# Attention followed by a SoLU layer, batch 0's preparation: 64-bit weights turned into float32 in another way, and the first units placed anew

## The chip, the core and the metric

The kernel runs on one core of a Trainium2 chip. A core has TensorE (PE; its weight loads are counted apart as PEld), VectorE (DVE), ScalarE (ACT), GpSimd (POOL) and SyncE (SP, which issues the DMAs here). Each engine works through its own instructions in a fixed order, and semaphores hold it where it needs another's result. The metric is the device time of one execution, in microseconds.

## The reference

Two attentions in a row: 32 packed tokens per head read the sequence, then the sequence reads the packed tokens. A layer with a SoLU and a layer norm follows. The sizes are batch B = 8, H = 8 heads, S = 576 rows, D = 64.

```python
p_packed = sm_attn(p, k, v)               # softmax(p k^T / 8) v, 32 rows per head
out = sm_attn(q, p_packed, p_packed)      # softmax(q p_packed^T / 8) p_packed
x = out.transpose(0, 2, 1, 3).reshape(4608, 512)
h = x @ w_in                              # 512 x 1024
e = np.exp(h - h.max(-1))
solu = h * e / (e.sum(-1) + 1e-9)
ln = (solu - mean) / np.sqrt(var + 1e-6) * g_ln
result = ln @ w_out                       # 1024 x 512
```

q, k, v, p and g_ln arrive as float32. w_in and w_out arrive as 64-bit floats: 512 x 1024 and 1024 x 512 of them, 4 MB each, seen by the kernel as pairs of 32-bit words (low word, high word).

## The kernel before

**Per batch.** `pack(b)` is the first attention: keys transposed (`kT`), scores on TensorE, softmax, the weights transposed (`e1T`), times v, giving `ppT`. `unpack(b)` is the second one: queries transposed (`qT`), scores, maxima per block of 32 (`mx`), POOL's or DVE's subtraction, an exponential on ACT (`a`), sums (`sm`), a product. It doesn't multiply by the packed values: it computes z = packed x w_in once (`zh`, and the rest `zl`), and the weights of the softmax, transposed (`a2h`, and the rest `a2l`), are then the left operand of `h`. Both are generators, and each `yield` ends a unit.

**Per tile of 128 rows.** `mlp_in` forms h with 12 matmuls (three products of high and low parts, two halves of the heads, two halves of the columns; 24 for a boundary tile, which holds 64 rows of each of two batches), its row maximum `nm` on DVE, an exponential `e` on ACT and u = e x h x a row factor on DVE. `mlp_norm` subtracts the mean and splits the result into two float16 parts `yhl` (the first on ACT, the second on DVE); a transposing DMA on SP makes `yT` of it. `mlp_out` multiplies yT by the scaled w_out (`wch`, and the rest `wcl`, both float16) with 24 matmuls, and DVE brings the result out of PSUM (`o_sb`). Tile i's output product runs some tiles after its h.

**Preparation, before the first tile.** Eight chunks of 128 x 1024 numbers, four of w_in and four of w_out, are turned from 64-bit words into float32, as high part (sign, exponent, 23 bits) and low part. `high_part` takes the high word: ACT scales it as a float32 by 2^-112 (L202), DVE shifts it by 3 and clears the sign bit (L204), and DVE puts the sign back (L205). `add_low_part` isolates the exponent on DVE (L212) and multiplies the low word by it, on DVE (L217) or on ACT and then POOL or DVE (L220, L221); the sum is formed on POOL or DVE (L233), or on TensorE as two products with an identity (L226, L227), which ACT copies back (L229). A digit of `HOW` per chunk says how: 0 for DVE alone up to 6. `prepare_w_out` then takes magnitudes on ACT (`mag`), sums them on TensorE, makes a power of two per column from the sum (`scale`, `inv`), scales by it and by g_ln (L321 on ACT, L322 on POOL or DVE), casts to float16 (L323) and takes the residual (L330).

**What sets the order.** A scheduler places each unit by its position in the program, shifted by the offset of the `high_priority` around it. Tables of offsets do this for batch 0's preparation (`PACK0`, `W_IN`, `UNPACK0`, `W_OUT`, `SCALE_AT`, `PARTS`). `FIRST_BATCH` says behind which tile of batch 0 each unit of batch 1's unpacking and batch 2's packing stands, and with which offset; `LATER` does so for the other batches. `LOADS` is the order of the first loads (w a chunk of w_in, o one of w_out, P the packed tokens of the later batches), and `FETCH` places the loads of later batches. All loads, transposing DMAs and stores are issued by SP in one queue. From batch 1 on TensorE's order is that of the program.

Buffers: `e`, `u`, `o_sb`, `zh`, `zl`, `yhl`, `yT` have two each, `mag` one, the PSUM tile `pa` three, `h` two. The raw words of w_in and of two chunks of w_out lie in the tiles `zh` and `zl`, those of the other two in `raw`, which k and q share (three of them).

## Time and profile before

| | |
|---|---|
| median of 3 runs | 468.33 us (467.21 to 469.08) |
| the profiled execution | 468.75 us, span 466.9 us |
| granted TensorE clock, mean | 0.952 |
| busy TensorE (PE) | 429.6 us, 92% of the span |
| busy VectorE (DVE) | 355.1 us, 76% |
| weight loads (PEld) | 236.3 us, 51% |
| busy ScalarE (ACT) | 231.2 us, 50% |
| busy GpSimd (POOL) | 143.4 us, 31% |

Shares are over the whole span, and the first 150 us differ from the rest: there the weights are prepared and batch 0 and half of batch 1 are set up, and the engines take turns as the one that is waited for. So what follows reads stretches of the span and single marks in it. A group's row gives line, engine, operation, output and inputs, partitions x elements, count, then busy time and mean ns of one, then idle time ahead of it and what ended it.

### The profile page before, as it was taken

The numbers are of one execution on the slowest core, as the hardware profiler recorded it, in microseconds if no ns is written. First come the engines' busy times: TensorE is split into PE (matmuls) and PEld (weight loads), VectorE is DVE, ScalarE is ACT, GpSimd is POOL, SyncE is SP. The second block draws the span as 40 slices with busy tenths as digits, with TensorE's granted clock in tenths as the row PEclk, the third lists the DMA queues.
The fourth block names the chain that finished last, engine by engine and source line by source line (L and its number), as shares of the span: only waits on it lengthen the run. The fifth ranks groups of instructions, "written<-read, shape, count | busy, mean of one in ns | idle before, by whom it ended". The sixth has DMA issues, their size and how long they took to land.

```text
span 466.9 us, 8257 instructions
## 1 busy us (share of the span) xinstructions
PE 429.6 (92%) x3116; PEld 236.3 (51%) x3116; DVE 355.1 (76%) x649; ACT 231.2 (50%) x403; POOL 143.4 (31%) x243
## 2 busy tenths in 40 slices
PE   9698577977978999999999999999999999999995
PEld 7472235733344455456644554566445545565542
DVE  4567999887774998998489989984898687566651
ACT  3477747763341556366346563663466444444430
POOL 2325467923200513321015123210152242212220
PEclk9889657898997999999999999999999999999999
DMA  9999999999949949989969489357433324435442
GB/s 267 338 268 286 155 191 132 128 184 173 153 103 186 142 97 160 224 128 157 176 140 144 97 155 183 77 119 178 69 67 69 76 62 113 90 67 125 80 115 65
DMA packets 237880, 67.00 MB, mean 143 GB/s; under 512 B 208912, under 2 KB 231440, under 8 KB 237328
## 3 DMA queue, kind: packets, MB, share of 16 engines
q1 hardware_dynamic: 237840, 66.48, 75.8%
q8 instruction: 24, 0.39, 0.4%
q14 instruction: 16, 0.13, 0.1%
HBM read 37.23 MB, written 9.44 MB: 100 GB/s over the span
## 4 chain that ended last, share of the span: by engine, by line
PE 38%; DVE 31%; ACT 9%; issue 7%; DMA 7%; POOL 4%; SPq 2%; DVEq 0%; POOLq 0%; ACTq 0%
PE po L564 21%; PE h L521 12%; DVE nm L523 4%; ACT yhl L544 3%; DMA zh<-in_moe_w_in_dram 3%; DVE qT L428 3%; DVE kT L350 3%; DVE u L534 3%; DVE zl L500 3%; ACT e L549 2%; DVE yhl L545 2%; DVE mx L443 2%; DVE sm L448 2%; PE pa L407 1%; PE pa L467 1%
## 5 line engine op out<-in xcount | busy, mean ns | idle before, releaser
L564 PE MATMUL po<-wch,yT 128*128 128x512 f16 x576 | 182.7, 382 | 5.9 <-DVE o_sb L566 4.8
L564 PEld LDWEIGHTS <-yT 128*128 128x128 f16 x864 | 81.0, 98 | 115.2 <-issue 24.7
L564 PE MATMUL po<-wcl,yT 128*128 128x512 f16 x288 | 109.7, 381 | 0.0
L521 PE MATMUL h<-zh,a2h 128*128 128x512 f32 x160 | 70.2, 439 | 1.8 <-DVE u L534 1.5
L531 ACT ACTIVATE e<-h,nm 128x1024 f32<-128x1024 f32 x36 | 40.1, 1115 | 58.1 <-DVE nm L523 57.6
L544 ACT ACTIVATE yhl<-u,negmu 128x1024 f16<-128x1024 f32 x36 | 41.4, 1149 | 50.9 <-POOL negmu L542 47.2
L521 PE MATMUL h<-zh,a2l 128*128 128x512 f32 x160 | 64.4, 403 | 0.0
L521 PE MATMUL h<-zl,a2h 128*128 128x512 f32 x160 | 64.2, 401 | 0.0
L545 DVE SCALAR_TENSOR_TENSOR yhl<-u,negmu,yhl 128x1024 f16<-128x1024 f32 x36 | 46.4, 1288 | 17.4 <-ACT yhl L544 17.3
L534 DVE SCALAR_TENSOR_TENSOR u<-e,s_row,h 128x1024 f32<-128x1024 f32 x36 | 46.0, 1277 | 9.8 <-ACT e L531 8.6
L523 DVE TENSOR_REDUCE nm<-h 128x1 f32<-128x1024 f32 x36 | 43.6, 1212 | 11.7 <-PE h L521 11.6
L566 DVE SCALAR_TENSOR_TENSOR o_sb<-po,c_row,inv 128x512 f32<-128x512 f32 x36 | 26.8, 745 | 26.1 <-PE po L564 26.1
L551 POOL TENSOR_SCALAR s_eps<-se,s_row 128x1 f32<-128x1 f32 x36 | 10.7, 297 | 102.2 <-ACT e L531 65.3
L554 POOL TENSOR_SCALAR c_row<-sq,s_eps 128x1 f32<-128x1 f32 x36 | 15.7, 437 | 82.9 <-ACT e L549 82.9
L549 ACT ACTIVATE e<-u,negmu 128x1024 f32<-128x1024 f32 x36 | 40.9, 1136 | 0.0
L521 PEld LDWEIGHTS h<-zh,a2h 128*128 128x128 f32 x160 | 31.1, 194 | 18.9 <-issue 9.0
L521 PEld LDWEIGHTS h<-zh,a2l 128*128 128x128 f32 x160 | 30.8, 193 | 7.9 <-issue 0.5
L521 PEld LDWEIGHTS h<-zl,a2h 128*128 128x128 f32 x160 | 31.1, 194 | 6.0
L444 POOL TENSOR_TENSOR s<-s,mx 128x576 f32<-128x576 f32 x14 | 16.0, 1160 | 49.3 <-DVE mx L443 49.3
L446 ACT ACTIVATE a<-s 128x576 f32<-128x576 f32 x16 | 10.9, 684 | 30.6 <-POOL s L444 28.1
L508 DVE TENSOR_TENSOR a2l<-s,a2h 128x576 fp32r<-128x576 f32 x16 | 14.0, 881 | 13.1 <-ACT a2h L507 13.1
L381 ACT ACTIVATE e<-pa,nmx 128x288 f32<-128x288 f32 x28 | 13.7, 496 | 19.4 <-DVE nmx L373 10.8
(139 smaller groups left out, 614.1 us busy)
## 6 DMA issues: line engine op xcount, KB each, us to landing
out_dram<-o_sb SPq DMA_DIRECT2D x36, 256.0 KB, 2.1
v_sb<-in_v_dram SPq DMA_DIRECT2D x16, 512.0 KB, 6.0
raw<-in_k_dram SPq DMA_DIRECT2D x28, 288.0 KB, 6.4
raw<-in_q_dram SPq DMA_DIRECT2D x96, 72.0 KB, 2.8
zh<-in_moe_w_in_dram SPq DMA_DIRECT2D x2, 1024.0 KB, 7.0
zl<-in_moe_w_in_dram SPq DMA_DIRECT2D x2, 1024.0 KB, 8.4
raw<-in_q_dram SPq DMA_DIRECT2D x4, 512.0 KB, 9.3
raw<-in_moe_w_out_dram SPq DMA_DIRECT2D x2, 1024.0 KB, 6.0
```

The costliest lines, as they stand in the source:

```text
L350: nc.vector.transpose(out=kT[:, g], in_=kraw[:, g].rearrange('p a i -> p (a i)'))
L444: eng.tensor_tensor(out=s2[r], in0=s2[r], in1=mx.unsqueeze(2).broadcast_to([P, NB, J]), op=ALU.subtract)
L521: nc.tensor.matmul(h[:, 512 * n:512 * n + 512], lhsT=lhsT, rhs=z[:, r, 512 * n:512 * n + 512], start=t == 0, stop=t == len(terms) - 1)
L523: nc.vector.tensor_reduce(out=nm, in_=h, axis=AX.X, op=ALU.max, negate=True)
L531: nc.scalar.activation(e, h, AF.Exp, bias=nm, accum_out=se)
L534: nc.vector.scalar_tensor_tensor(out=u, in0=e, scalar=s_row, in1=h, op0=ALU.mult, op1=ALU.mult, accum_out=su)
L544: nc.scalar.activation(yhl[:, 0], u, AF.Identity, bias=negmu)
L545: nc.vector.scalar_tensor_tensor(out=yhl[:, 1], in0=u, scalar=negmu, in1=yhl[:, 0], op0=ALU.add, op1=ALU.subtract)
L549: nc.scalar.activation(e, u, AF.Square, bias=negmu, accum_out=sq)
L554: nc.gpsimd.tensor_scalar(out=c_row, in0=sq, scalar1=1.0 / DF, scalar2=s_eps, op0=ALU.mult, op1=ALU.add)
L564: nc.tensor.matmul(po, lhsT=yT[:, a, c], rhs=w[:, c], start=c == 0 and t == 0, stop=c == NFC - 1 and t == 2)
L566: nc.vector.scalar_tensor_tensor(out=o_sb, in0=po, scalar=c_row, in1=inv, op0=ALU.mult, op1=ALU.mult)
```

## The change

The high part takes two full-width instructions instead of three: ACT scales by 2^-112 with Prelu, whose slope for negative inputs is 2^32, and DVE shifts the bits by 3; the slope leaves the sign bit where the shift puts it in its place. `low_part` makes the exponent out of ACT's bits with a shift and a mask in one DVE instruction (L209), and multiplies it by the low word, on DVE for six chunks (L211, `HOW` 'd') or on ACT (L213, in place) and POOL (L214) for two ('p'). The sum of high and low part is formed on TensorE for all eight chunks (`whole`, L224 and L225), where it was for three. ACT copies it back for w_in (L579) and for four of the eight pieces of w_out (L301). The other four, marked 'x' in `SCALED_BY`, DVE scales by both factors straight out of PSUM (L313). The residuals of w_out (L323) are all on DVE, where three were on POOL; of the scalings that aren't 'x', two are on POOL instead of seven. The low parts of the last two chunks get a tile of their own (`spare_rest`, of the tag `zl`). All tables of batch 0 have new numbers.

```diff
-HOW = '42313324'
-SCALED_BY = 'pppppdpp'
-REST_BY = 'pdddppdd'
-ZL_BY = 'pppp'
-A2L_BY = 'dd'
+HOW = 'dddddpdp'
+SCALED_BY = 'dppxxpxx'
+REST_BY = 'dddddddd'
+ZL_BY = 'pppd'
+A2L_BY = 'dp'
...
-FIRST_BATCH = [[3, 3, 3, 5, 6, 11, 15], [6, 6, 8, 8, 10, 15, 16, 16, 16], ...
+FIRST_BATCH = [[1, 2, 2, 2, 4, 4, 12], [9, 12, 14, 20, 20, 20, 21, 24, 24], ...
...
-FETCH = [[['k', 0, 0], ['v', 0, 0], ['q', 0, 0]], ...
+FETCH = [[['k', 0, 500], ['v', 0, 500], ['q', 1, -200]], ...
...
         bits = mlp.tile([P, DF], F32, name='e', bufs=2)
-        nc.scalar.activation(bits, hi.bitcast(F32), AF.Copy, scale=2.0 ** (-112))
-        bits = bits.bitcast(I32)
-        nc.vector.tensor_scalar(out=bits, in0=bits, scalar1=3, scalar2=2147483647, op0=ALU.logical_shift_left, op1=ALU.bitwise_and)
-        return nc.vector.scalar_tensor_tensor(out=dst.bitcast(I32), in0=hi, scalar=-2147483648, in1=bits, op0=ALU.bitwise_and, op1=ALU.bitwise_or)
+        nc.scalar.activation(bits, hi.bitcast(F32), AF.Prelu, scale=2.0 ** (-112), alpha=2.0 ** 32)
+        nc.vector.tensor_scalar(out=dst.bitcast(I32), in0=bits.bitcast(I32), scalar1=3, scalar2=None, op0=ALU.logical_shift_left)
+        return bits
+
+    def low_part(bits, raw, chunk, rest):
         lo, _ = words_of(raw)
-        ...
+        nc.vector.tensor_scalar(out=bits.bitcast(I32), in0=bits.bitcast(I32), scalar1=3, scalar2=-8388608, op0=ALU.logical_shift_left, op1=ALU.bitwise_and)
+        if HOW[chunk] == 'd':
+            nc.vector.scalar_tensor_tensor(out=rest, in0=lo.bitcast(U32), scalar=2.0 ** (-52), in1=bits, op0=ALU.mult, op1=ALU.mult)
+        else:
+            nc.scalar.activation(lo.bitcast(F32), lo.bitcast(U32), AF.Copy, scale=2.0 ** (-52))
+            EN(nc, HOW[chunk]).tensor_tensor(out=rest, in0=lo.bitcast(F32), in1=bits, op=ALU.mult)
+        return rest
...
+    def whole(high, rest, i):
+        half = slice(512 * i, 512 * i + 512)
+        ps = ps_a.tile([P, 512], F32, name='pa')
+        nc.tensor.matmul(ps, lhsT=ident, rhs=high[:, half], start=True, stop=False)
+        nc.tensor.matmul(ps, lhsT=ident_r, rhs=rest[:, half], start=False, stop=True)
+        return ps
...
             with tc.high_priority(offset=W_OUT[n][2]):
-                add_low_part(wg[n], w_out_raw[n], 4 + n, g_sb[:, 2 * n:2 * n + 2])
+                rests[n] = low_part(rests[n], w_out_raw[n], 4 + n, rest_tile() if n < 2 else spare_rest[:, n - 2])
+                for i in range(2):
+                    if SCALED_BY[2 * n + i] != 'x':
+                        w = wg[n][:, i * DM:(i + 1) * DM]
+                        nc.scalar.activation(w, whole(wg[n], rests[n], i), AF.Copy, scale=g_sb[:, 2 * n + i:2 * n + i + 1])
...
-                if how == 's' and (not scaled):
-                    nc.vector.scalar_tensor_tensor(out=w, in0=w, scalar=g_sb[:, c:c + 1], in1=scale, op0=ALU.mult, op1=ALU.mult)
+                if SCALED_BY[c] == 'x':
+                    nc.vector.scalar_tensor_tensor(out=w, in0=whole(wg[c // 2], rests[c // 2], c % 2), scalar=g_sb[:, c:c + 1], in1=scale, op0=ALU.mult, op1=ALU.mult)
                 else:
-                    ...
+                    EN(nc, SCALED_BY[c]).tensor_tensor(out=w, in0=w, in1=scale, op=ALU.mult)
```

**Where the instructions stand.** First SP's queue, before, from the third chunk of w_out on: v and k of batch 1 (`v_sb`, `raw`), packed p (`pT`), q of batch 1.

```order
L138 DMA raw<-in_moe_w_out_dram 128x2x1024
L138 DMA zh<-in_moe_w_out_dram 128x2x1024
L107 DMA v_sb<-in_v_dram 128x8x128 x2
L134 DMA v_sb<-in_v_dram 64x8x64
L96 DMA raw<-in_k_dram 32x72x32 x4
L272 DMA pT_84<-p2t 64x896 x4
L107 DMA raw<-in_q_dram 128x8x128 x2
L115 DMA raw<-in_q_dram 64x4x64 x2
```

SP's queue after, from the same place:

```order
L138 DMA raw<-in_moe_w_out_dram 128x2x1024
L107 DMA v_sb<-in_v_dram 128x8x128 x2
L134 DMA v_sb<-in_v_dram 64x8x64
L138 DMA zh<-in_moe_w_out_dram 128x2x1024
L265 DMA pT_84<-p2t 64x896 x4
L96 DMA raw<-in_k_dram 32x72x32
L107 DMA raw<-in_q_dram 128x8x128
L96 DMA raw<-in_k_dram 32x72x32
L107 DMA raw<-in_q_dram 128x8x128
L115 DMA raw<-in_q_dram 64x4x64
L96 DMA raw<-in_k_dram 32x72x32 x2
L115 DMA raw<-in_q_dram 64x4x64
```

The last chunk of w_out moved behind v, and the four parts of k moved behind packed p and between the parts of q. Ahead of this stretch, w_out's first chunk moved from behind q of batch 0 to ahead of it.

ACT before, from the high part of w_in's last chunk (read from `zl`) on; L398 copies the packing weights of batch 0, L128 and L129 its queries:

```order
L202 ACTIVATE e<-zl 128x1024
L220 ACTIVATE u<-zh 128x1024
L398 COPY e1T<-pa 64x256
L398 COPY e1T<-pa 128x512
L128 COPY qT<-h 128x2x2x128
L129 COPY qT<-h 128x64
L128 COPY qT<-h 128x2x2x128
L129 COPY qT<-h 128x64
L202 ACTIVATE e<-raw 128x1024
```

ACT after, from the same instruction on:

```order
L202 ACTIVATE e<-zl 128x1024
L390 COPY e1T<-pa 128x512
L390 COPY e1T<-pa 64x256
L213 ACTIVATE zh<-zh 128x1024
L579 COPY w_in_sb<-pa 128x512
L260 ACTIVATE p2raw<-p2raw 128x896
L579 COPY w_in_sb<-pa 128x512
L128 COPY qT<-h 128x2x2x128
L129 COPY qT<-h 128x64
```

The low part of w_out's second chunk (L213) moved ahead of the copies of w_in, the scaling of packed p (L260) and the copies of the queries.

DVE before, around the first output tile (`o_sb`, L566); L439, L443 and L448 belong to the unpacking of batch 1:

```order
L439 STREAM_TRANSPOSE s_889<-pa 128x288
L439 STREAM_TRANSPOSE s_890<-pa 128x288
L545 SCALAR_TENSOR_TENSOR yhl<-u,negmu,yhl 128x1024
L439 STREAM_TRANSPOSE s_889<-pa 128x288
L443 TENSOR_REDUCE mx<-s_889 128x18
L545 SCALAR_TENSOR_TENSOR yhl<-u,negmu,yhl 128x1024
L566 SCALAR_TENSOR_TENSOR o_sb<-po,c_row,inv 128x512
L439 STREAM_TRANSPOSE s_890<-pa 128x288
L428 STREAM_TRANSPOSE qT<-raw 128x576 x4
```

DVE after, from the first output tile on:

```order
L558 SCALAR_TENSOR_TENSOR o_sb<-po,c_row,inv 128x512
L515 TENSOR_REDUCE nm<-h 128x1
L407 COPY ppT<-pa 128x128
L517 TENSOR_SCALAR bound<-nm 128x1
L518 TENSOR_SCALAR bound<-nm,bound 128x1
L520 RECIPROCAL s_row<-bound 128x1
L526 SCALAR_TENSOR_TENSOR u,su<-e,s_row,h 128x1024
L537 SCALAR_TENSOR_TENSOR yhl<-u,negmu,yhl 128x1024
L431 STREAM_TRANSPOSE s_878<-pa 128x288
L431 STREAM_TRANSPOSE s_879<-pa 128x288
L431 STREAM_TRANSPOSE s_878<-pa 128x288
L558 SCALAR_TENSOR_TENSOR o_sb<-po,c_row,inv 128x512
```

The first output tile moved ahead of the unpacking's transposes, of a row maximum and of a yhl; the second one stands among the transposes now, where the first one stood.

From about the row maximum of the boundary tile between batches 0 and 1 on, the orders of both kernels are the same: of the changed kernel's instructions these are the last 2561 of 3184 on TensorE, 442 of 616 on DVE, 179 of 298 on ACT and 192 of 231 on POOL. The table of activation functions is loaded once in both.

More of the change, by code (lines that the diff above doesn't have):

```diff
@@ L201, in high_part @@
         bits = mlp.tile([P, DF], F32, name='e', bufs=2)
-        nc.scalar.activation(bits, hi.bitcast(F32), AF.Copy, scale=2.0 ** (-112))
-        bits = bits.bitcast(I32)
-        nc.vector.tensor_scalar(out=bits, in0=bits, scalar1=3, scalar2=2147483647, op0=ALU.logical_shift_left, op1=ALU.bitwise_and)
-        return nc.vector.scalar_tensor_tensor(out=dst.bitcast(I32), in0=hi, scalar=-2147483648, in1=bits, op0=ALU.bitwise_and, op1=ALU.bitwise_or)
-    def add_low_part(dst, raw, chunk, factors=None):
-        how = HOW[chunk]
-        lo, _ = words_of(raw)
-        power = mlp.tile([P, DF], F32, name='u', bufs=2)
-        nc.vector.tensor_scalar(out=power.bitcast(I32), in0=dst.bitcast(I32), scalar1=-8388608, scalar2=None, op0=ALU.bitwise_and)
-        rest = power
-        if how in '36':
-            rest = mlp.tile([P, DF], F32R, name='u', bufs=2)
-        if how in '026':
-            nc.vector.scalar_tensor_tensor(out=rest, in0=lo.bitcast(U32), scalar=2.0 ** (-52), in1=power, op0=ALU.mult, op1=ALU.mult)
-        else:
-            low = rest if how == '3' else mlp.tile([P, DF], F32, name='u', bufs=2)
-            nc.scalar.activation(low, lo.bitcast(U32), AF.Copy, scale=2.0 ** (-52))
-            EN(nc, 'd' if how in '45' else 'p').tensor_tensor(out=rest, in0=low.bitcast(F32) if how == '3' else low, in1=power, op=ALU.mult)
-        if how in '36':
-            for i in range(2):
-                half = slice(512 * i, 512 * i + 512)
-                ps = ps_a.tile([P, 512], F32, name='pa')
-                nc.tensor.matmul(ps, lhsT=ident, rhs=dst[:, half], start=True, stop=False)
-                nc.tensor.matmul(ps, lhsT=ident_r, rhs=rest[:, half], start=False, stop=True)
-                if factors is None:
-                    nc.scalar.copy(dst[:, half], ps)
-                else:
-                    nc.scalar.activation(dst[:, half], ps, AF.Copy, scale=factors[:, i:i + 1])
-        else:
-            EN(nc, 'p' if how in '124' else 'd').tensor_tensor(out=dst, in0=dst, in1=rest, op=ALU.add)
@@ L330, in prepare_w_out @@
                     EN(nc, REST_BY[c]).tensor_tensor(out=wcl[:, c], in0=w, in1=wch[:, c], op=ALU.subtract)
-        return last.ins
     def pair(b):
@@ L582, in packed_attention_solu_kernel @@
         with tc.high_priority(offset=W_IN[g][0]):
-            high_part(w_in_sb[:, g], w_in_raw[g], g)
+            bits = high_part(w_in_sb[:, g], w_in_raw[g], g)
         with tc.high_priority(offset=W_IN[g][1]):
-            add_low_part(w_in_sb[:, g], w_in_raw[g], g)
+            bits = low_part(bits, w_in_raw[g], g, rest_tile())
+            for i in range(2):
+                nc.scalar.copy(w_in_sb[:, g, 512 * i:512 * i + 512], whole(w_in_sb[:, g], bits, i))
+    spare_rest = par.tile([P, 2 * DF], F32R, name='zl', bufs=2).rearrange('p (n f) -> p n f', n=2)
     keep_busy(*BUSY[1])
```

33 lines of the change are left out of this document (15 added, 18 removed).

## The prediction

> **What bounds the kernel now.** I read first the busy time by stretches (columns: length; busy PE, weight load, DVE, ACT, POOL with their counts; granted clock; DMA share; GB/s).
>
> ```profile
> 36.00:48.00 12.00, 9.56 (x75) 2.40 (x74) 10.12 (x11) 9.75 (x12) 7.44 (x3) 1.00 1.01 290
> 48.00:60.00 12.00, 7.03 (x12) 2.67 (x11) 12.00 (x17) 9.49 (x16) 5.75 (x4) 0.64 1.18 165
> 60.00:72.00 12.00, 8.93 (x44) 4.52 (x44) 11.96 (x16) 5.45 (x10) 5.78 (x4) 0.50 1.14 176
> 300.00:400.00 100.00, 99.07 (x730) 54.10 (x728) 77.20 (x151) 50.71 (x89) 25.64 (x58) 1.00 0.42 91
> ```
>
> From 300 to 400 us TensorE is busy 99.07 of 100: there only its work counts, and the change leaves that work and its order alone. From 48 to 72 us DVE is busy 23.96 of 24 and PE idles 8: the preparation is bound by DVE. So the change is worth what it moves the moment at which batch 0 hands over. Second came the chain of waits, for marks on the way there (start, length, what), and one ACT row.
>
> ```profile
> 62.61 2.67 DVE kT L350 x4
> 95.88 4.65 DMA yT<-yhl
> 112.37 0.76 DVE o_sb L566
> 133.79 1.23 DVE nm L523
> ```
> ```profile
> 109.93 1.15 ACT L544 ACTIVATE yhl<-u,negmu 128x1024 f16<-128x1024 f32 x1 [3.71 <-DMA yT<-yhl]
> ```
>
> The marks: K, where batch 1's keys are transposed on DVE (62.6); T, where the first tile's transposed activations have landed (95.88 + 4.65 = 100.5); O, where the first output tile has left PSUM and the second output product may start (112.37 + 0.76 = 113.1); N, the maximum over the boundary tile (133.8). After N the orders are the same, so the shift of N is the forecast. O is late because its DVE instruction stands behind a yhl that waits, through ACT (idle 3.71), for a transposing DMA.
>
> **The change on DVE.** Its prices are taken from undisturbed instructions (the first fence: line, operation, count, busy, mean ns, idle before):
>
> ```profile
> L204 DVE TENSOR_SCALAR e<-e 128x1024 int32<-128x1024 int32 x8 | 7.2, 894 | 8.7 <-ACT e L202 8.7
> L212 DVE TENSOR_SCALAR u<-w_in_sb 128x1024 int32<-128x1024 int32 x4 | 2.8, 695 | 2.3 <-POOL u L221 2.3
> L205 DVE SCALAR_TENSOR_TENSOR w_in_sb<-zh,e 128x1024 int32<-128x1024 int32 x2 | 2.5, 1225 | 0.1
> L221 POOL TENSOR_TENSOR u<-u 128x1024 fp32r<-128x1024 f32 (+1 forms) x4 | 10.2, 2550 | 22.5 <-ACT u L220 15.0 <-DVE sm L449 6.2 <-DVE mx L443 1.3
> L322 POOL TENSOR_TENSOR yhl<-yhl,o_sb 128x512 f32<-128x512 f32 x4 | 6.6, 1671 | 3.3 <-DVE o_sb L310 3.3
> ```
> ```profile
> 45.82 2.38 POOL L221 TENSOR_TENSOR u<-u 128x1024 fp32r<-128x1024 f32 x1 [1.27 <-DVE mx L443]
> 46.08 3.19 DVE L205 SCALAR_TENSOR_TENSOR yT<-raw,e 128x1024 int32<-128x1024 int32 x1
> 93.53 0.67 DVE L330 TENSOR_TENSOR wcl<-yhl,wch 128x512 f16<-128x512 f32 x1
> 34.82 0.28 DVE L415 COPY ppT<-pa 128x128 f32<-128x128 f32 x1
> 83.92 1.23 DVE L534 SCALAR_TENSOR_TENSOR u<-e,s_row,h 128x1024 f32<-128x1024 f32 x1
> ```
>
> A chunk costs DVE 0.69 + 1.23 + 0.69 now and 2 x 0.69 after: 8 x 1.23 = 9.8 saved. Low-part products on DVE go from 4 to 6: +2.5. Four scalings out of PSUM are new (between 0.67, all in SBUF, and the 0.76 of o_sb, out of PSUM; I take 0.74, its nearest kin): +3.0. Residuals on DVE go from 5 to 8: +2.0; one zl comes, one a2l goes. Sum: -2.3 us of clean work.
>
> The larger part is POOL. It loses 9 full-width instructions, 4 scalings, 3 residuals and one zl, and gets 2 low products and one a2l: 9 x 2.55 + 8 x 1.67 - 2 x 2.55 - 1.67 = 29.5 us less. What this gives DVE: the L205 at 46.08 took 3.19 instead of 1.23 while POOL ran from 45.82 to 48.20, and the eight L204 have a mean of 0.894 against 0.695. The Trainium skill (SBUF — State Buffer, "Who interferes with whom") says that a VectorE instruction with two SBUF inputs and a GpSimd instruction that reads SBUF exclude each other for a whole instruction; 48.20 + 1.23 = 49.43 against the measured end 49.27, so this trace agrees.
>
> Both parts together, counted on the queue. From the copy of ppT (ends 35.1) to the end of the first u (85.15) DVE has now 50 us, nearly all busy. After, the same stretch holds all eight residuals (three now) and full width 4 x 1.23 + 8 x 0.69 + a p2t of about 1.1 + nm 1.23 + u 1.23 = 14.0, 33 instructions of 512 or 576 columns at 0.67 (three scale steps at an estimated 0.4, four scalings at 0.74) = 21.6, seven of 288 at about 0.4 = 2.8, ten tiny ones about 1: 39 us. If DVE never waited, the u would end 11 us earlier. It will wait:
>
> **What is late next.** ACT and the queue of loads (SP), each in order.
>
> ```profile
> 35.86 1.13 ACT L202 ACTIVATE e<-zh 128x1024 f32<-128x1024 f32 x1 [1.31 <-DMA zh<-in_moe_w_out_dram]
> 37.51 0.56 ACT L229 COPY w_in_sb<-pa 128x512 f32<-128x512 f32 x1
> 49.98 0.68 ACT L446 ACTIVATE a<-s 128x576 f32<-128x576 f32 x1 [2.48 <-DVE s L444]
> 26.00:28.00 2.00, 2.00 (x35) 1.50 (x33) 1.41 (x2) 2.00 (x4) 0.35 (x1) 0.65 0.37 21
> ```
> ```profile
> 36.58 0.40 SPq L138 DMA_DIRECT2D zh<-in_moe_w_out_dram  x1
> zh<-in_moe_w_out_dram SPq DMA_DIRECT2D x1, 1024.0 KB, 9.1
> 40.38 5.16 SPq L134 DMA_DIRECT2D v_sb<-in_v_dram  x1
> v_sb<-in_v_dram SPq DMA_DIRECT2D x1, 128.0 KB, 9.9
> 51.58 1.63 SPq L96 DMA_DIRECT2D raw<-in_k_dram  x1
> raw<-in_k_dram SPq DMA_DIRECT2D x1, 288.0 KB, 6.4
> 61.55 0.65 SPq L115 DMA_DIRECT2D raw<-in_q_dram  x1
> raw<-in_q_dram SPq DMA_DIRECT2D x1, 64.0 KB, 4.3
> ```
>
> On ACT the low part of w_out's second chunk (in zh, landed at 35.86) now stands ahead of the w_in copies, the scaling of p and all q copies: ACT idles from about 27.4 until that load. Behind it, by widths at 0.5 to 1.05 from start to start: eight w_in copies 4.0, four signs (Prelu) 4.2, two low parts 2.1, p 0.9, q copies 2.5, magnitudes 2.5, w_out copies 1.9: 18.1 us; then about 2 us of waiting for the last w_out chunk, which now comes after v (v cost 50.3 - 45.7 = 4.6 us of queue). So batch 0's softmax exponentials start at 54 to 56 instead of 49.98, and DVE reaches the keys at about 60.5 instead of 62.6. Prelu itself is in no row: between the copy's 1.13 and, say, twice that; I take 1.13, as the same words pass; at twice, four lie in this chain, +4.5 us, of which the next wait hides 3.5.
>
> The keys are not there. Now they land at 51.58 + 6.4 = 58.0, ahead of packed p and q, whose last part lands at 61.55 + 4.3 = 65.85. After, their four parts stand behind packed p and between the four of q; only a 64 KB part of q is behind them. Equal bytes in a queue that is full end them at 65.85, less the gap of 26 to 28 us (21 GB/s now), which is likely filled, as w_out's first chunk is issued ahead of q: 64.0 to 65.9. I take 64.0: **K moves by +1.4**, and DVE's relief up to there is gone.
>
> From K to the end of u: 22.5 us now. After: 20.4 of the 39 us, 2.3 for a loop (a2l on DVE, four matmuls in queue, the last magnitude, then DVE's scale), 1.5 for three POOL scalings beside it (5.0 us of POOL; 0 to 5.0): 24.2. End of u: 88.2, +3.0.
>
> **Given back behind u.** SP and PE prices:
>
> ```profile
> 73.35 8.99 SPq L85 DMA_DIRECT2D raw<-in_q_dram  x12
> 90.30 5.48 SPq L85 DMA_DIRECT2D raw<-in_q_dram  x6
> 95.88 3.08 SPq L547 DMA_TRANSPOSE yT<-yhl  x1
> 33.88 1.02 PE L226 MATMUL pa<-w_in_sb,ident 128*128 128x512 f32 x2
> 34.97 1.02 PE L226 MATMUL pa<-w_in_sb,ident 128*128 128x512 f32 x2
> 143.94 0.63 PE L521 MATMUL h<-zh,a2l 128*128 128x512 f32 x1
> ```
>
> No residual is left after u. nm and batch 2's keys take 4.4 us, then three q parts on SP (0.75 to 0.91 each, 2.5), then the transposing DMA: T = 88.2 + 4.4 + 2.5 + 4.65 = 99.75, -0.8. The second transpose follows after 3.1 + 8 x 0.83 = 9.7 us and lands at 109.4. The first output tile no longer stands behind the waiting yhl: its 24 products end before that, so O = 109.4, -3.7.
>
> From O to N: 20.7 now, all PE work. After, batch 1's unpacking scores stand behind 22 of the second product's 24 matmuls; from there a chain of o_sb, maximum, four q transposes, second maximum, POOL's subtraction, exponential, sums, POOL's product, transpose and a2l ends 20.9 us after O, and 13 matmuls at 0.23 follow: 23.9, +3.2. Sum: 1.4 + 1.6 - 3.8 - 2.9 + 3.2 = **-0.5 us at N**.
>
> Ten identity pairs more on PE (34.97 - 33.88 = 1.09 each, 10.9 us) cost nothing: PE waits in that stretch for ACT and DVE, 10.5 us from 36 to 72 as it is; were that cover gone, up to 10.9.
>
> The profiled execution took 468.75 us, 0.42 above the median 468.33. So 468.75 - 0.5, less 0.42: **467.8 us**.
>
> **Rivals.** (1) The relief arrives, faster. If the keys land before DVE reaches them (60.5), the wait of 3.5 us goes: 464.3; if the unpacking also hides behind PE's 20.7 us, another 3.2: 461. For it: SP's queue had a gap. Against: the rows of the queue above. (2) The keys later, slower: every us after 64.0 moves N one to one, at 66.9 the run is 2.8 us longer than my forecast, out of the band; with 68 it is 471.8. For it: the parts of q ahead of them; against: equal bytes. (3) POOL's three scalings block DVE's in-order queue for their whole 5.0 us instead of 1.5: 471.3. The L205 row speaks for it, that some of DVE's operands there are in PSUM against it; it decides from 2.8 us lost. By the rule of SBUF — State Buffer in the Trainium skill, this is the price where both operands of DVE's instruction are in SBUF. (4) PE idles about 5 us ahead of the 13 matmuls, and they run at 0.43 as the one at 143.94 (0.63 with its pipeline, next start 0.43 later) does: +2.6, 470.4. The Trainium skill (TensorE: Matmul & The Clock Gate, "Part 1") says an idle window of about 3.4 us halves the clock; the 0.50 of 60 to 72 us agrees.
>
> **How the numbers follow.** About 0.5% (2.3 us: 466.0 to 470.7) is what this measurement can tell from no change. Forecast 0.32 (own range 466 to 470); rival 1 0.40, in two steps of 0.22 and 0.18, each less likely than the forecast; rival 2 0.15; rival 3 0.09; rival 4 0.04, inside the band. Faster 0.40, same 0.36, slower 0.24. The range leaves out a part of the 461 and what goes past 472: 460.5 to 472.5.
>
> **What would show it.** DVE waits some 3 us for batch 1's keys, which start at 64 to 66; ACT idles from 27 to 35; POOL under 20 us up to 100; the first transposed tile lands near 99.8, the second product starts near 109.4, N comes near 133.3. It is wrong if the keys start below 61 or above 67, if Prelu rows are not near 1.13, or if PE is busy all through the unpacking.

## The result: slower by 0.8%, and the profile after

The changed kernel takes 472.55 us (median of 9 runs, 470.48 to 474.40), the kernel before 468.41 us (9 runs, 467.21 to 471.00). The ratio is 1.0081, with a 95% interval from 1.0053 to 1.0108: 4.1 us slower. The forecast was 467.8 us, half a microsecond faster than before, with a range of 460.5 to 472.5; the time lies 0.05 us above the range. The profiled execution, 470.48 us with a span of 468.6 us, is the fastest of its nine. A second profile of the same code (472.99 us, span 470.4 us) is nearer to the median, and stands beside it where the difference matters.

First the busy time by stretches, the same ones as before (columns: length; busy PE, weight load, DVE, ACT, POOL; granted clock; DMA share; GB/s).

```profile
26.00:28.00 2.00, 2.00 (x57) 1.42 (x60) 1.39 (x2) 0.85 (x3) 0.00 (x0) 0.50 1.21 292
36.00:48.00 12.00, 10.59 (x59) 5.19 (x58) 7.19 (x9) 10.48 (x21) 0.88 (x1) 1.00 1.07 309
48.00:60.00 12.00, 11.51 (x77) 4.05 (x76) 10.57 (x17) 9.38 (x15) 2.37 (x2) 1.00 1.11 195
60.00:72.00 12.00, 7.49 (x28) 4.01 (x28) 8.35 (x12) 6.27 (x11) 8.01 (x5) 0.76 1.45 145
300.00:400.00 100.00, 99.07 (x729) 54.34 (x727) 78.18 (x155) 50.63 (x88) 25.59 (x59) 1.00 0.44 92
```

The stretch from 300 to 400 us is as it was. From 48 to 72 us DVE is busy 18.92 of 24 us, where it was busy 23.96: its relief is there, and turned into waiting. POOL does 34 us up to 156 us, where it did 64. Now the marks on DVE and SP in the timeline (start, length, engine, line, instruction, idle time ahead and what ended it):

```profile
64.96 2.76 DVE L342 STREAM_TRANSPOSE kT<-raw 128x576 f32<-128x576 f32 x4 [2.60 <-issue]
73.83 0.69 DVE L304 TENSOR_SCALAR o_sb<-po 128x512 f32<-128x512 f32 x1 [2.89 <-PE po L295]
86.87 1.27 DVE L526 SCALAR_TENSOR_TENSOR u<-e,s_row,h 128x1024 f32<-128x1024 f32 x1
93.90 2.05 SPq L539 DMA_TRANSPOSE yT<-yhl  x1
108.36 0.75 DVE L558 SCALAR_TENSOR_TENSOR o_sb<-po,c_row,inv 128x512 f32<-128x512 f32 x1 [4.13 <-PE po L556]
137.15 1.22 DVE L515 TENSOR_REDUCE nm<-h 128x1 f32<-128x1024 f32 x1 [0.70 <-PE h L513]
149.42 1.23 DVE L515 TENSOR_REDUCE nm<-h 128x1 f32<-128x1024 f32 x1 [3.64 <-PE h L513]
```

Batch 1's keys (K) start at 65.0 instead of 62.6, the column scale's first step at 73.8 instead of 69.8, the first u at 86.9 instead of 83.9, the first output tile (O) leaves PSUM at 109.1 instead of 113.1, and the boundary tile's maximum (N) comes at 137.15 instead of 133.79. The next row maximum, the last row here, came at 147.80 before and comes at 149.42.

That last pair gives the shortest account of the result. Up to this maximum both kernels have done the same products, except that the changed one has summed ten more pieces on TensorE (30 matmuls). One row each for before and after, from the start to that maximum:

```profile
0.00:147.80 147.80, 118.24 (x953) 68.31 (x961) 109.93 (x181) 79.57 (x145) 61.64 (x64) 0.85 1.05 197
```
```profile
0.00:149.42 149.42, 125.23 (x983) 71.52 (x991) 96.58 (x182) 74.99 (x142) 32.82 (x50) 0.90 1.02 192
```

TensorE's busy time grew by 6.99 us and its idle time fell by 5.37 (29.56 to 24.19): 1.62 us later. The second profile of the changed code has 125.23 us busy and 25.92 idle, and comes to this maximum at 151.15, 3.35 us later than before. Behind this maximum all 20 profiles of this study take 319.1 to 319.9 us to the end, so it is a mark that can be compared between the kernels.

### The profile page after: what moved, and what is told of

Its sections match the earlier page's. It is cut to its first block, busy times and chain, and to the rows that moved or that the text cites. A ratio compares the mean times of both kernels' runs of the same rounds, so it can differ in the third digit from the quotient of the medians.

```text
span 468.6 us, 8288 instructions
## 1 busy us (share of the span) xinstructions
PE 436.6 (93%) x3146; PEld 239.6 (51%) x3146; DVE 341.9 (73%) x650; ACT 226.6 (48%) x400; POOL 114.4 (24%) x229
## 4 chain that ended last, share of the span: by engine, by line
PE 38%; DVE 34%; ACT 9%; SPq 8%; issue 7%; DMA 3%; POOL 1%; DVEq 0%; ACTq 0%
PE po L556 18%; PE h L513 12%; DVE nm L515 4%; DVE kT L342 4%; ACT yhl L536 4%; DVE qT L420 3%; SPq L107 3%; DVE u L526 3%; DVE zl L492 3%; DVE yhl L537 2%; ACT e L541 2%; DVE sm L440 2%; DVE mx L363 2%; DVE mx L435 2%; SPq L115 1%
## 5 line engine op out<-in xcount | busy, mean ns | idle before, releaser
L513 PEld LDWEIGHTS h<-zh,a2h 128*128 128x128 f32 x160 | 31.5, 197 | 22.6 <-issue 7.1
L389 PE MATMUL pa<-ident,e 128*128 128x128 f32 (+1 forms) x80 | 15.0, 324 | 7.9 <-ACT e L373 7.7
```

Of the source, the lines that this page charges most:

```text
L513: nc.tensor.matmul(h[:, 512 * n:512 * n + 512], lhsT=lhsT, rhs=z[:, r, 512 * n:512 * n + 512], start=t == 0, stop=t == len(terms) - 1)
```

## The experiments

All ratios are against the kernel before, run on the same chip in the same comparison. Over the six comparisons the median of the kernel before was 467.96 to 468.89 us, so a difference of times from two comparisons can be off by about 1 us for this alone. Ten of the eighteen measured times lie outside every range that was stated for them: these runs rule theories out more than they confirm one.

**1. Again, and the tables taken back.** The changed code as it is; the changed code with the old `FIRST_BATCH`; and with nine tables of numbers old. In the third kernel the arithmetic, the letters that say which engine does what, and `LOADS`, the order of the first loads (the first chunk of w_out ahead of batch 0's queries), are still new.

```diff
-FIRST_BATCH = [[1, 2, 2, 2, 4, 4, 12], [9, 12, 14, 20, 20, 20, 21, 24, 24], ...
+FIRST_BATCH = [[3, 3, 3, 5, 6, 11, 15], [6, 6, 8, 8, 10, 15, 16, 16, 16], ...
 (third kernel: PACK0, W_IN, UNPACK0, W_OUT, SCALE_AT, CHUNKS, PARTS, FETCH old too)
```

> The changed kernel itself, unchanged, for a second trace: the profiled execution shown took 470.48 us, the fastest of nine with a median of 472.55. If what the trace shows (+1.7 us at the row maximum of the second tile behind the boundary, 149.4 against 147.8) is the whole effect, the median comes out near 470.5 here. If single executions lose another 2 us in stretches that PE runs at half clock, the median is 472 to 473 again, and a profiled execution above 472 has longer such stretches before 150 us, with the same order and the same wait elsewhere.

> The changed kernel with the old table of where batch 0's tiles take the units of batch 1's unpacking and batch 2's packing. Theory placement: the loss was made behind the first u, where the unpacking of batch 1 came late and PE waited and ran at half clock; with the old table 468 to 470. Theory preparation: the loss was made ahead of the first tile (keys at 65.0 instead of 62.5, first u at 88.2 instead of 85.2); the table changes nothing, 472 to 473.

> The changed kernel's new arithmetic with all nine tables of batch 0's placement old: the arithmetic alone. Theory placement: near the kernel before or faster, 464 to 468, since DVE has 2.3 us and POOL 29.5 us less work. Theory preparation: the new arithmetic with its waits on ACT and its late magnitudes costs by itself, 471 to 475.

Measured: 472.96 us (1.0097 [1.0066, 1.0129]), 480.90 us (1.0295 [1.0259, 1.0332]) and 481.13 us (1.0277 [1.0238, 1.0316]). The result repeats. The new arithmetic with the old tables is 13.2 us slower than the kernel before (481.13 less the 467.96 of the same comparison), and `FIRST_BATCH` alone carries nearly all of the difference between the tables (480.90 against 481.13). With the old tables N itself is hardly later than in the changed kernel (137.72 against 137.15), but the next maximum comes 20.6 us behind it instead of 12.3; a row of TensorE in the timeline of the kernel with all tables old shows the wait between them:

```profile
142.75 2.47 PE L389 MATMUL pa<-ident,e 128*128 128x128 f32 x9 [4.13 <-ACT e L373]
```

There the packing of batch 2 starts behind N, and TensorE waits for its exponentials. So N alone is not a safe finishing line: what stands right behind it has to be read with it.

**2. A warm TensorE ahead of the boundary tile.** Ten products more, whose result is overwritten, keep TensorE busy in the wait ahead of it.

```diff
+                if warm_first and n == 0 and t == 6:
+                    for _ in range(WARM):
+                        nc.tensor.matmul(h[:, 512:1024], lhsT=terms[0][0], rhs=zl[1][:, 0, 512:1024], start=True, stop=True)
```

> The changed kernel with ten extra products of TensorE ahead of batch 1's share of the boundary tile (their result is overwritten), in the stretch where PE idles from 125.9 to 128.2 us and then runs at half clock until 134.7. Theory half clock: the 18 products behind the idle stretch and the two groups among them go from 8.9 to about 7 us, the row maximum behind them from 137.2 to about 135.2, and 1 to 2 us are won at the end, 470.5 to 471.5. Theory preparation: what counts is the chain through DVE, no gain: 472 to 473.

Measured: 472.04 us (1.0076 [1.0048, 1.0103]). In the changed kernel TensorE idles 2.27 us ahead of these products, and they then start about 0.43 us apart until 134.3, and 0.23 apart behind that:

```profile
128.19 0.80 PE L513 MATMUL h<-zh,a2h 128*128 128x512 f32 x1 [2.27 <-ACT a2h L499]
131.05 0.63 PE L513 MATMUL h<-zh,a2h 128*128 128x512 f32 x1
131.47 0.63 PE L513 MATMUL h<-zl,a2h 128*128 128x512 f32 x1
134.67 0.40 PE L513 MATMUL h<-zh,a2l 128*128 128x512 f32 x1
134.91 0.39 PE L513 MATMUL h<-zh,a2h 128*128 128x512 f32 x1
```

With the ten products the boundary tile runs at 0.23, and N comes 1.7 us earlier than in the second profile (137.17 against 138.88), though the keys start as late there (66.10). But the next stretch, which is slow in the changed kernel too (144.8 to 148.3), is slow for longer (145.0 to 150.6):

```profile
127.99 2.56 PE L517 MATMUL h<-zl,a2h 128*128 128x512 f32 x10
135.93 0.39 PE L518 MATMUL h<-zh,a2l 128*128 128x512 f32 x1
147.21 0.63 PE L518 MATMUL h<-zh,a2l 128*128 128x512 f32 x1
147.63 0.63 PE L518 MATMUL h<-zh,a2h 128*128 128x512 f32 x1
```

The half clock cost N about 1.7 us; counted from O it was 2.1 (25.9 us from O to N, against 28.0 in both profiles of the changed kernel). The next maximum comes 14.1 us behind N instead of 12.3, so nearly all of it is lost again, and the run is 0.9 us faster than the changed kernel in the same comparison, within the intervals.

**3. Batch 1's keys earlier, and later, in SP's queue.**

```diff
-        prefetch(1, what, 0)
+        prefetch(1, what, 600 if what == 'k' else 0)      # keys first
+        prefetch(1, what, 400 if what == 'q' else 0)      # keys last
```

> The changed kernel with the four parts of batch 1's keys issued ahead of its queries on SP (DVE's transposes of them then stand ahead of the second half of batch 0's softmax; else the same order). Theory keys: DVE's wait for the keys carries the loss, and from the keys on to the row maximum of the second tile behind the boundary both kernels take the same 84.5 to 85.3 us. Here the keys start near 61.5 instead of 65.0 to 66.4, and 2 to 4 us are won: 468.5 to 470.5. Theory downstream: the loss comes from the order behind the first u and from half-clock stretches, an earlier start is eaten up there: 472 to 473.

> The changed kernel with the queries of batch 1 ahead of the last three parts of its keys on SP; on DVE only two instructions behind the keys change places. Theory keys: the keys land 0.5 to 3 us later than in the changed kernel, and the end moves by as much, 473 to 476. Theory downstream: no change, 472 to 473.

Measured: 471.89 us (1.0083 [1.0052, 1.0115]) and 473.33 us (1.0096 [1.0072, 1.0120]). With the keys first, DVE starts them at 59.94 instead of 64.96 to 66.39, and the first row maximum comes at 75.33 instead of 75.77 to 77.58: 5 to 6.5 us of keys moved it by 0.4 to 2.2 us. So issuing the keys first, on which the forecast's first term rested, doesn't win back the 4 us. It doesn't price the keys' landing alone, though: with the keys first DVE's transposes of them also stand ahead of the second half of batch 0's softmax. The run with the keys last prices nothing: its keys start at 65.30, between the 64.96 and 66.39 of the two profiles of the changed kernel, and that its time lies in the range of the theory "keys" is chance. One reason why earlier keys are worth little stands in TensorE's timeline of the changed kernel, and in DVE's row of the first piece that is read out:

```profile
78.61 1.13 PE L224 MATMUL pa<-yhl,ident 128*128 128x512 f32 x2
79.17 0.80 PE L225 MATMUL pa<-zl,ident_r 128*128 128x512 f32 x1
79.90 0.93 PE L360 MATMUL pa<-kT,pT 64*32 64x288 f32 x16
```
```profile
76.90 0.74 DVE L313 SCALAR_TENSOR_TENSOR yhl<-pa,g_sb,o_sb 128x512 f32<-128x512 f32 x1
```

The sums of the 'x' pieces (L224, L225) lie in the PSUM tiles `pa` until DVE has the column scale and reads them out. There are three such tiles, and the packing scores of batch 1 (L360) need them: they start at 79.90, 15 us behind their keys. Before, they started right behind them:

```profile
63.35 2.96 PE L368 MATMUL pa<-kT,pT 64*32 64x288 f32 x17 [3.07 <-DVE kT L350]
```

**4. The two halves of the change, each alone.** The kernel before with all nine new tables; the kernel before with the old tables and only the high part by Prelu and a shift; and the new tables with the Prelu part.

```diff
-        nc.scalar.activation(bits, hi.bitcast(F32), AF.Copy, scale=2.0 ** (-112))
-        ...
+        nc.scalar.activation(bits, hi.bitcast(F32), AF.Prelu, scale=2.0 ** (-112), alpha=2.0 ** 32)
+        return nc.vector.tensor_scalar(out=dst.bitcast(I32), in0=bits.bitcast(I32), scalar1=3, scalar2=None, op0=ALU.logical_shift_left)
```

> The kernel before, its old arithmetic, with the nine new tables of placement (the loads of batch 1 keep the old order on SP: keys ahead). If the new tables are the better placement whatever the arithmetic, 465 to 468. If they only suit the arithmetic they came with, over 472, as the old tables under the new arithmetic (481).

> The kernel before with one part of the change alone: Prelu and one shift make the high part, eight times 1.2 us less on DVE; low parts, sums and tables are the old ones. If DVE's work ahead of the keys bounds the old kernel as its trace says, and the placement holds, up to 5 us faster: 463 to 467. If a shorter instruction only lets DVE wait for the next load or for POOL's sums, 467 to 469; if the scheduler's placement falls apart as it did for the whole arithmetic under the old tables, over 472.

> The old arithmetic with the new tables (463.8 us), and of the new arithmetic Prelu and the shift alone. If the 9.8 us that DVE no longer works are on the path there, 459 to 462; if DVE only waits longer for POOL and for loads, 463 to 465; if the scheduler's order gets worse as under the old tables (+3.3), over 466.

Measured: **463.80 us (0.9899 [0.9863, 0.9934])** for the new tables alone, the fastest kernel of this study; 471.65 us (1.0066 [1.0040, 1.0092]) for Prelu with the old tables; 466.08 us (0.9951 [0.9935, 0.9968]) for Prelu with the new ones. So the placement gains 4.6 us and the rest of the change loses 8.8 (472.6 less 463.8), of which the Prelu part is 2.3; by the intervals each of these two losses is uncertain by about 2 us. The rest is called the arithmetic below, but it holds two things more: the letters that hand work from one engine to another, and the place of w_out's first chunk in `LOADS`, which is old in the kernels with the old arithmetic and new in those with the new one. No run takes `LOADS` back alone. That it does something can be seen: in the changed kernel TensorE waits 0.70 us for batch 0's queries (`raw<-in_q_dram`) at 30.82, and in the kernel before it doesn't wait for them. The same window as above, for the new tables alone:

```profile
0.00:142.65 142.65, 118.41 (x953) 69.76 (x961) 106.03 (x180) 79.63 (x145) 63.02 (x64) 0.84 1.02 203
```

TensorE's idle time is 24.24 us, as in the changed kernel (24.19). The changed kernel's TensorE is busy 6.82 us longer, and its row maximum comes 6.77 us later; in its second profile it comes 8.50 us later, 6.82 of busy time and 1.68 of idle time.

Busy time alone understates what the sums take. Counted in the timeline from each product's start to the next one's (or to its own end, where TensorE idles behind it), the sums take 20.33 us of TensorE in the changed kernel (48 products), 7.92 in the kernel with the new tables alone and 9.16 in the kernel before (18 products each). So they grew by 12.4 us against the same tables, while the other products together took 5.6 us less, at a granted clock of 0.90 instead of 0.84 up to that mark.

The Prelu part takes work off DVE (351.2 to 345.0 us over the span) and adds none to TensorE, yet loses. Where, the rows of SP and of TensorE show; first with the new tables and Prelu, then with the new tables alone (L562 and L564 are the output product):

```profile
86.06 10.67 SPq L85 DMA_DIRECT2D raw<-in_q_dram  x15
96.83 5.28 SPq L545 DMA_TRANSPOSE yT<-yhl  x2
102.07 0.61 PE L562 MATMUL po<-wch,yT 128*128 128x512 f16 x1 [7.37 <-DMA yT<-yhl]
```
```profile
86.89 9.31 SPq L85 DMA_DIRECT2D raw<-in_q_dram  x13
96.30 2.37 SPq L547 DMA_TRANSPOSE yT<-yhl  x1
100.91 0.39 PE L564 MATMUL po<-wch,yT 128*128 128x512 f16 x1 [1.28 <-DMA yT<-yhl]
```

Buffers come free earlier, so 15 parts of a later batch's queries instead of 13 stand ahead of the first transposing DMA, and it is no earlier than without the relief (96.83 against 96.30). TensorE, whose products of h are done sooner, idles 7.37 us for it instead of 1.28, and starts behind that at half clock; the first output tile comes at 110.09 instead of 106.61. With the old tables the same stands in SP's queue: eight parts instead of six, and 98.30 instead of 95.88. How much of the 2.3 to 3.3 us this carries was not measured apart.

**5. No piece, or one, scaled out of PSUM.**

```diff
-SCALED_BY = 'dppxxpxx'
+SCALED_BY = 'dppddpdd'      # no x;  one x: 'dppddpdx'
```

> The changed kernel with no piece of w_out scaled out of PSUM: ACT copies the sums of the four 'x' pieces out, times g_ln, as it does those of the others, and DVE scales them in SBUF. Theory banks: in the changed kernel the sums of three 'x' pieces hold all three PSUM tiles 'pa' from about 65 us until the column scale is known (76.9 to 81.3), so that the scores of batch 1's packing start 12 to 15 us behind its keys (79.9 to 81.7, against 63.4 behind 62.5 in the kernel before), its ppT comes at 110 to 112 instead of 97, and batch 1's unpacking ends late. Without 'x' the scores start within 5 us of the keys' transposes, ppT comes at 97 to 103, and 4 to 7 us are won: 466 to 468.5. Theory keys alone: the late keys carry the loss, and this changes nothing: 472 to 473.

> As the kernel without 'x', but with the last piece (7) still scaled out of PSUM, which holds one of the three tiles 'pa'. Theory banks: two tiles are left for the scores, the first three of four groups start early, and most of the gain stays: 466.5 to 470. Theory keys alone: 472 to 473.

> No 'x', and batch 1's keys issued ahead of its queries. Theory banks: the keys' 5 us, worth only 1 us while the scores waited for PSUM, count once the banks are free: 1.5 to 4 us faster than the kernel without 'x'. If DVE's and ACT's order behind the keys bounds instead, within 1 us of it.

Measured: 472.91 us (1.0099 [1.0079, 1.0118]), 473.80 us (1.0109 [1.0078, 1.0141]), and 473.46 us (1.0118 [1.0095, 1.0141]) with the keys first as well. The held tiles are gone, and the time is the same. TensorE and SP without an 'x':

```profile
67.79 1.99 PE L360 MATMUL pa<-kT,pT 64*32 64x288 f32 x8
```
```profile
92.16 11.68 SPq L85 DMA_DIRECT2D raw<-in_q_dram  x16
103.94 2.49 SPq L539 DMA_TRANSPOSE yT<-yhl  x1
```

The scores follow their keys now (66.30) within 1.5 us, and batch 1's packed values come at 103.5 instead of 110.2. But the unpacking that frees the query tiles is earlier too, so all 16 parts of batch 3's queries stand ahead of the first transposing DMA, which is issued at 103.94 instead of 93.90, and O comes at 119.3 instead of 109.1. One wait was exchanged for another. With one 'x' it is the same (scores at 68.52, packed values at 103.1, transposing DMA at 103.60).

**6. Batch 3's queries held back.** A POOL copy that needs the second tile's row factor writes into the tile that these queries are loaded into, so their DMAs can't stand ahead of the first transposing ones. In the kernel without 'x', in the changed kernel, and in the kernel before with the new tables. The same edit moves the place of these loads in the program (`FETCH`) from ahead of batch 1's fourth tile to ahead of its first, so it isn't the hold alone.

```diff
-FETCH = ... ['q', 3, 1000]], ...
+FETCH = ... ['q', 0, 1000]], ...
...
+            nc.gpsimd.tensor_copy(raw[:, :, 0, 0], behind.broadcast_to([P, G]))
...
+                elif b == 3:
+                    loaded['q', b] = load_x(q[b], crows[1])
```

> No 'x', and the loads of batch 3's queries wait (for the second tile's row factor, through a copy of four columns on POOL), so that they no longer stand ahead of the first two transposing DMAs on SP. Theory two chains: the boundary tile's row maximum comes 27 us after ppT or 20.3 us after the first output tile, whichever is later. ppT stays at 103.5, the first transposing DMA goes out near 97 instead of 104, the first output tile comes at 109 to 111 instead of 118.6, the boundary maximum near 131 instead of 138.8, and 5 to 8 us are won over the kernel without 'x': 465 to 468. If another limit lies just behind (the arithmetic's order on DVE and ACT), 471 to 473.

> The changed kernel with batch 3's queries held back in the same way, 'x' kept. Theory two chains: ppT at 110 to 112 sets the end, and the queue had only three parts ahead of the first transposing DMA; at most 1 us, 471.5 to 473. If the queue alone is the limit of the new arithmetic, 465 to 469.

> The old arithmetic with the new tables (463.8 us), and batch 3's queries held back. Theory two chains: ppT is at 96.4 there (27 us later is 123.4), the first transposing DMA stands 4.6 us behind its yhl, and the boundary maximum at 128.3 is set by the first output tile; with the queue free it comes near 124, and 2 to 5 us are won: 459 to 462. If the second chain isn't the limit, 463 to 464.5.

Measured: 472.91 us (1.0099 [1.0073, 1.0125]), 471.37 us (1.0062 [1.0037, 1.0087]) and 466.47 us (0.9961 [0.9942, 0.9981]). Without 'x', DVE starts on the first output tile 10.7 us earlier (107.92 against 118.58), and the end stays where it was: now DVE's transposes of the queries wait for the parts that were held back, and TensorE waits 3.39 us behind them. In the changed kernel N comes at 134.87 in a profiled execution that is 3 us faster than its median, and 1.2 us may be won; in the kernel with the new tables alone 2.7 us are lost. So the queue is one wait among several, and taking it away brought little or nothing.

**7. ACT's wait, and the sums by themselves.** All low products on DVE and the scaling of packed p on POOL, so that ACT has no load to wait for ahead of batch 0's queries; the same without an 'x'; and the kernel before with the new tables (463.8 us), with its high part formed in the old way, but all eight sums on TensorE and all low products on DVE.

```diff
-HOW = 'dddddpdp'
+HOW = 'dddddddd'
-        nc.scalar.mul(raw, raw, SCALE)
+        nc.gpsimd.tensor_scalar(out=raw, in0=raw, scalar1=SCALE, scalar2=None, op0=ALU.mult)
 (second kernel: SCALED_BY = 'dppddpdd' too)
 (third kernel, of the kernel before with the new tables:)
-HOW = '42313324'
+HOW = '66666666'
```

> The changed kernel with all eight low products on DVE and the scaling of packed p on POOL: ACT has no longer an instruction that waits for a load of w_out (the low part L213, idle 7.67 us there) ahead of the copies of batch 0's queries. If ACT's wait carries the rest of the loss: batch 0's exponentials start near 51 to 52 us instead of 56, the column scale near 70 instead of 73.8 to 75.6, the boundary tile's maximum 2 to 4 us earlier than in the changed kernel, and 467 to 470 us in all. If the wait hides behind the keys and the held PSUM tiles: exponentials earlier, but the packed values of batch 1 still at 109 to 112 and 472 to 473 us.

> The same, and besides no piece is scaled out of PSUM (SCALED_BY 'dppddpdd'), so the sums do not hold PSUM tiles for the column scale. If the two waits together carry the loss (each hiding the other): the packing scores right behind the keys, packed values of batch 1 before 102 us, 464 to 468 us. If a third wait (the first transposing DMA behind batch 3's queries on SP, as without the x pieces alone) decides: transposing DMA after 101 us, and 471 to 474 us.

> The kernel before with all nine new tables (463.8 us), but all eight low products on DVE and all eight sums on TensorE with ACT's copies behind them (HOW '66666666'); the sign as before, no piece scaled out of PSUM at the end. If the move of the sums to TensorE and ACT carries the part of the arithmetic's loss that the Prelu does not (8.8 less 2.3, so 6.5 us): 468 to 472 us, with ACT's exponentials of batch 0 later by 3 us or more. If that part is the pieces held in PSUM and the waiting low part on ACT, which this kernel lacks: 463 to 466 us.

Measured: 475.33 us (1.0129 [1.0107, 1.0151]), 471.50 us (1.0070 [1.0031, 1.0109]) and 480.09 us (1.0230 [1.0192, 1.0268]). ACT's rows, of the changed kernel and then of the first of these three:

```profile
34.52 1.18 ACT L213 ACTIVATE zh<-zh 128x1024 f32<-128x1024 uint32 x1 [7.67 <-DMA zh<-in_moe_w_out_dram]
56.23 0.68 ACT L438 ACTIVATE a<-s 128x576 f32<-128x576 f32 x1 [0.33 <-DVE s L436]
```
```profile
34.61 0.58 ACT L579 COPY w_in_sb<-pa 128x512 f32<-128x512 f32 x1 [7.40 <-PE pa L225]
55.77 0.68 ACT L438 ACTIVATE a<-s 128x576 f32<-128x576 f32 x1 [0.33 <-DVE s L436]
```

The wait for the load had lain beside a wait of the same length for TensorE: its sums of w_in stand behind batch 0's last packing products and 30 products that transpose queries. The exponentials come half a microsecond earlier, not 4 to 5 as one of the theories had it, and the time is outside both ranges. N comes at 133.79 in that kernel, 3.4 us earlier, and the next maximum at 153.47, 4.1 us later, as in the kernels with old tables and with the same wait (TensorE's 4.13 us for batch 2's exponentials). Without an 'x' as well, the scores follow their keys (67.09) and the packed values come at 98.5, but the first transposing DMA is issued at 102.89, as in experiment 5, and O comes at 119.1.

The third kernel is slower than both theories allowed, and it is no clean test of the sums: low products moved from POOL to DVE with them, the order came out differently, the last chunk of w_out was issued behind batch 1's keys, and ACT waited 5.17 us for it.

```profile
60.71 1.14 ACT L202 ACTIVATE e<-zh 128x1024 f32<-128x1024 f32 x1 [5.17 <-DMA zh<-in_moe_w_out_dram]
```

What it shares with every kernel that has its sums on TensorE is that engine's account up to the row maximum behind the boundary tile, worked out from windows like those above:

| kernel | maximum at, us | PE busy | PE idle |
|---|---|---|---|
| before | 147.80 | 118.24 | 29.56 |
| before, new tables | 142.65 | 118.41 | 24.24 |
| the same with Prelu | 146.46 | 117.55 | 28.91 |
| changed | 149.42 | 125.23 | 24.19 |
| changed, second profile | 151.15 | 125.23 | 25.92 |
| changed, old tables | 158.31 | 126.32 | 31.99 |
| changed, no x | 151.88 | 125.08 | 26.80 |
| changed, queries held back | 147.13 | 124.59 | 22.54 |
| low products on DVE | 153.47 | 126.80 | 26.67 |
| low products on DVE, no x | 146.18 | 123.64 | 22.54 |
| new tables, sums on TensorE | 158.14 | 130.87 | 27.27 |

Over all 20 profiles, the five without the ten additional sums have 117.3 to 118.5 us of busy TensorE there, the fifteen with them 123.6 to 130.9. The idle time into which the additional work was to fall is 22.5 us at best: no order tried brought it under 22, and the fastest kernel has 24.2 without the additional work. The two rows with 22.5 are of executions 3 to 4 us faster than their kernels' medians (468.36 against 471.37, 467.84 against 471.50). All this is an account, not a proof that taking the sums off TensorE gives back 6.8 us, since no kernel was run that differs in these sums alone with the order unchanged.

## Why the prediction was wrong, step by step

- **Up to O most of it held, and O itself by luck.** DVE was relieved as counted (idle where it was full), POOL a little less (23.8 us up to 100, under 20 forecast), ACT idled from 26.85 to 34.52 (forecast 27 to 35), Prelu took 1.15 us a chunk (1.13 taken), the scaling out of PSUM 0.74 (0.74). The keys came at 65.0 in one profile and 66.4 in the other (64.0), the end of u at 88.14 and 89.95 (88.2), O at 109.1 and 110.9 (109.4). The exponentials came at 56.23 (54 to 56). But O was forecast as the landing of the second transposed tile, with the first output tile done before it. That tile landed at 106.3, and O came from the first output product, for which DVE waited 4.13 us; the two errors met at nearly the same number.
- **The step that failed is "From O to N ... 23.9":** it took 28.0 us. The forecast's chain, up to the last a2l, ended 22.6 us behind O (20.9 forecast), and the products behind it took 5.4 us instead of 3.0: they ran at half clock until 134.3, and a group of batch 2's packing scores, which the forecast hadn't counted, stands among them (132.0 to 133.2). The half clock was rival 4, held at 0.04; by the run with the ten warming products, which takes 25.9 us from O to N, it was about 2.1 us of the 4.1. The forecast had put its condition at an idle time of about 5 us; 2.27 us were enough.
- **"After N the orders are the same, so the shift of N is the forecast" was too simple.** N moved by +3.36 in the profiled execution, the next maximum by +1.62, the span by +1.7; in the second profile by +5.09, +3.35 and +3.4. With the old tables it went the other way: N at 137.72, hardly later than in the changed kernel, and the end 8.6 us later. The mark has to be one behind which neither the order nor an open wait differs; the next maximum was one.
- **"Ten identity pairs more on PE ... cost nothing"** is a mis-sized term. It was given 0, with 10.9 as the price if its cover were gone. Of the cover that was named, 10.5 us of idle PE from 36 to 72 us, 6.4 are still idle after the change (36 less 10.59, 11.51 and 7.49): TensorE's busy time there grew by 4.1 us. Up to the row maximum the sums took 11.2 us more than before, so the price of 10.9 was about right. Against the kernel with the same tables, TensorE's idle time to that maximum did not shrink at all (24.24 there; 24.19 and 25.92 in the two profiles of the changed kernel), and its busy time grew by 6.8; that this is less than the 12.4 us which the sums took more goes with the other products, 5.6 us shorter at the higher clock. My reading, which no run shows by itself: the sums stand in the chain from the loads over ACT to the queries and the column scale, so the engines behind TensorE wait longer by what is added, and TensorE waits for them in turn.
- **The tiles `pa` were not in the forecast.** Four sums waiting in three PSUM tiles for the scale delayed batch 1's scores by 15 us. Taking the wait away gave nothing back, as the runs without 'x' show, because then the transposing DMA's place in SP's queue gave the same end. But it took worth out of earlier keys, in which rival 1 (0.40) saw its gain.
- **Rival 2, keys later one to one,** fits the difference between the two profiles of the changed code: keys at 64.96 and 66.39, and every mark behind them 1.7 to 1.8 us apart. The other way its price didn't hold: keys 5 to 6.5 us earlier, with DVE's order changed by it, gave 0.4 to 2.2 us at the first maximum.
- **Rival 3, POOL blocking DVE,** showed in another place than named, and there it hit waiting time. In the changed kernel:

```profile
47.12 2.66 POOL L214 TENSOR_TENSOR u<-zh,e 128x1024 fp32r<-128x1024 f32 x1 [43.60 <-PE pa L225]
```
```profile
47.54 2.79 DVE L209 TENSOR_SCALAR e<-e 128x1024 int32<-128x1024 int32 x1
```

POOL ends at 49.78, and 0.69 us later, the price of an undisturbed L209, would be 50.47; it ended at 50.33. The Trainium skill (SBUF — State Buffer, "Who interferes with whom") says that a `tensor_scalar` in its faster mode shares the port with GpSimd, and this row agrees. The three scalings feared at the column scale (three, not two as the section on the change has it) lost little: DVE's L313 beside them reads PSUM and took 0.74, its one L315 took 1.20.
- **"The preparation is bound by DVE" went too far.** The Prelu part alone takes eight times 1.23 us off DVE, and both kernels that have it alone are slower for it, by 2.3 and 3.3 us. A busy share of 23.96 in 24 us didn't say what DVE's work was worth.
- **The placement and the arithmetic were summed as one.** Alone, the new tables gain 4.6 us; the new arithmetic (with the new `LOADS`), which takes 9 us off DVE and 30 off POOL up to the row maximum, loses 8.8 with them and 13.2 with the old ones. The forecast didn't price the two apart.

**What stays open.** Of the 8.8 us, 2.3 go with the Prelu part, and SP's queue is the mechanism seen there, not shown to be all of it. The other 6.5 are a difference, uncertain by about 2 us. They lie near TensorE's additional 6.8 us, but that this is their cause is not shown: `LOADS` and the engines' letters are in them too, and the second profile has 1.7 us of idle time besides. None of the single waits that were taken away (the keys, the held PSUM tiles, ACT's load, the queue, the half clock) gave back more than 1.2 us against the changed kernel's median; wherever a wait went, another of nearly the same length stood beside it.

## What to carry to other kernels

Don't take work that is moved onto the engine which bounds the rest of the kernel as free because that engine idles nearby: compare its busy and idle time up to a mark behind which everything is the same, against a kernel with the same placement, and look whether the idle time shrinks. Relief for an engine that waits in turn with others brought nothing here, and it let transfers in earlier, which then stood in a queue ahead of the one that was waited for. When a change holds new arithmetic and a new placement, price them apart, since one can hide the other's sign: here the placement with the old arithmetic was the better kernel (0.990). And list all that differs before a run is called one part alone: here the order of the first loads went with the arithmetic.

## What the hardware showed that was not expected

- An idle time of 2.27 us on TensorE was followed by some 6 us at half clock (128.2 to 134.3 us), one of 2.95 us by as much (94.35 to 100.5 us). Ten products more in the first of these waits took that slow stretch away (0.23 us from start to start instead of 0.43); the next slow stretch, 144.8 to 148.3 without them, then lasted from 145.0 to 150.6.
- A leaky rectifier over 128x1024 float32 numbers of both signs took ACT 1.15 us, as long as the copy it replaced (1.13).
- A DVE instruction with one input in SBUF (L209) took 2.79 us instead of 0.69 beside a POOL product, while one with one of its two operands in PSUM (L313) kept its 0.74 us beside POOL's scalings.
